# Attention and a SiLU feed-forward on one core: where additions, squares, a transpose and a small matmul stand in the late couples

## The chip, the core and the metric

The kernel runs on one core of one Trainium2 chip. The metric is device time in microseconds (us) of one execution. The kernel before took 1332.61 us (median of three runs, 1331.04 to 1333.44).

## What is computed

```python
def rmsnorm(x, g):
    rms = np.sqrt(np.mean(x * x, axis=-1, keepdims=True) + 1e-06)
    return x / rms * g
q_n, k_n = (rmsnorm(q, g_q), rmsnorm(k, g_k))        # (8, 12, 448, 64): batch, heads, rows, width
scores = 1.0 / np.sqrt(64) * np.matmul(q_n, k_n.transpose(0, 1, 3, 2))
attn = softmax(scores)                                # over the last axis
x = np.matmul(attn, v)                                # then (B, H, S, D) -> (B*S, H*D) = (3584, 768)
h = x @ w_in                                          # (768, 2048)
g = h * (1.0 / (1.0 + np.exp(-h)))                    # SiLU
out = g @ w_out                                       # (2048, 768)
```
All of it is in fp32.

## The kernel before

**Couples.** The 96 heads of all batches are taken four at a time, as 24 *couples* (c = 0 to 23); six couples make a *group*, which is two batches. For each couple the main loop, at the end of `bounded`, calls `visit(c)` and then `between(c)`. I call the second a *stretch*. `GROUP` is 6 and `LATE` is 12.

**A visit** holds the attention of couple c. `scores(c, j, i)` makes four 64x64 matmuls into a PSUM tile named `sc`, of which there are two (L712), and ACT takes the exponential (L717), with the norm of k as its scale. `weigh` multiplies the exponentials with v into two PSUM banks named `av` (L749). The weighing of couple c - 1 ends in the visit of c: first `weigh(c - 1, LEFT)` and the first half of `weigh(c - 1, LEFT - 1)`, then `turn(1, ...)`, a copy of one column into a bank of `av` (L725; on ACT to couple 6, later on DVE), then `scores(c, 0, 1)`, then the second half of that weighing, for which PE waits on the copy. Then `divide` (L807, DVE) takes the result out of `av`, and the weighing of c starts in the same banks. Near the end two additions of exponentials (L763, `add(c, 1)`) go to DVE, and SP issues the loads of v.

**A stretch** holds two calls of `fill`. Each `fill` takes some 14 matmuls out of a generator that makes the products of the first feed-forward layer (L898), and deals other work between them. A list `others` is dealt evenly over the matmuls. A list `prompt` gives its first piece before the first matmul and one more after every third (`HW` is 3). What is dealt is put into its engine's queue at that point of the program, and each engine works its own queue in order.

**The products.** The first layer works by Strassen's scheme in Winograd's form: seven products, each of three matmuls of 128x128 with 448 columns, in the order 1, 2, 6, 5, 7, 3, 4, for each of eight blocks m of a group (`Seven`). The products take two PSUM banks named `mm` in turn, so a product needs that the one two before it has been taken out. ACT takes 1 and 5 out (L906, L916), DVE the others (L856); POOL makes two additions (L918, L919), and the eviction of product 3 reads what L918 wrote. Once the second product of a block has begun, ACT makes SiLU of the block before (L1036) and SP stores it (L931). A couple takes 28 matmuls of the 21 per block, so the stretches of three couples in a row start at three places in a block: couples 12, 15, 18, 21 at product 1, couples 13, 16, 19, 22 within product 6, couples 14, 17, 20, 23 within product 7.

**Late couples.** From couple 12 on q and k are transposed on DVE in place of PE (`flip`: L655 for q, L658 for k), k is scaled afterwards on ACT (`gain`, L664), and q's norm is made on the loaded tile: ACT squares (L672) and DVE adds (L673) in `sum_squares`; then `scale` joins the partial sums of partition pairs with a matmul against a constant (L684), DVE takes it out of its `sc` tile (L685), POOL raises it to the power -1/2 (L688) and multiplies q with it (L691). For k, `normalise` squares on ACT (L467), adds on DVE (L468, L492) and takes the power on POOL (L496), in two pieces, the second of which also issues the loads of the next k on SP (L282, L284).

**The order of a late stretch.** First q's transpose of couple c + 1 and the load of the next q. In the first `fill`: the evictions and the additions of the other exponentials (L763, four pieces) with the pieces of k of couple c + 2. In the second: the matmuls that sum the exponentials (L783), two reciprocals (L792) with the DMAs that spread them (L798, L800), k's transpose, then `gain` and `sum_squares(c + 2)` together. After both, and after the last products of a group with the sums of x (L853) that the next group needs, `scale(c + 2)`. Last comes a tiny exponential on ACT (L1501), ahead of which its table is loaded.

Of the kernel before, what the change touches and what calls it, by code (L numbers as in the profile page):

```python
# [13 lines left out]
ALU = mybir.AluOpType  # L14
# [521 lines left out]
def bounded(  # L536
# [3 lines left out]
    P, D, R, J, S = z.P, z.D, z.R, z.J, z.S  # L540
# [9 lines left out]
    GROUP, LATE = z.NPAIR, z.LATE  # L550
# [33 lines left out]
    n = 2 * room.COLS  # L584
# [13 lines left out]
    def q_of(c):  # L598
        return rows_q[c % 2 if c < GROUP else 0]
# [52 lines left out]
    def flip(c, name):  # L652

        if name == "q":
            nc.vector.transpose(qT.rearrange("p i s -> p (i s)"), q_of(c)[:, 0 : z.NK])  # L655
            load_q(c + 1)
            return
        nc.vector.transpose(kT, place["k1"])  # L658
        if c + 1 < NC:
            loads["quarters"](c + 1)  # L660
# [17 lines left out]
    def scale(c):  # L678

        if c >= NC:  # L680
            return
        f = norm.rms[c % 2][:, 0:n]
        t = ps.tile([P, 2, BANK], F32, name="sc", bufs=2)[:, 0, 0:n]
        nc.tensor.matmul(t, ident, f, start=True, stop=True)  # L684
        nc.vector.tensor_scalar(  # L685
            out=f, in0=t, scalar1=1.0 / D, scalar2=1e-6, op0=ALU.mult, op1=ALU.add
        )
        nc.gpsimd.tensor_tensor(out=f, in0=f, in1=minus_half.to_broadcast([P, n]), op=ALU.pow)  # L688
        rows = q_of(c)[:, 0 : z.NK].rearrange("p (n e) -> p n e", e=z.Q)
        factor = f.rearrange("p (n one) -> p n one", one=1).to_broadcast([P, n, z.Q])  # L690
        nc.gpsimd.tensor_tensor(out=rows, in0=rows, in1=factor, op=ALU.mult)  # L691

    def pair_up():

# [8 lines left out]
    def scores(c, j, i=None):  # L703


        two = ps.tile([P, 2, BANK], F32, name="sc", bufs=2)
        for half in range(2):
            pair = half if j == LEFT else i
            keys = kT[:, ds((z.KA, z.KB)[0 if j == LEFT else i] + j * P, P)]
            for h in range(2):  # L710
                rows = ds(h * D, D)
                nc.tensor.matmul(  # L712
                    two[ds(half * D, D), h, 0:S], keys[rows, ts(half, D)], qT[rows, pair, :],
                    start=True, stop=True,
                )
        for h in range(2):
            nc.scalar.activation(  # L717
                eleft[:, h] if j == LEFT else weights(c, j)[:, i, h], two[:, h, 0:S], AF.Exp,
                scale=norm.column(c, i, h, j),
            )  # L720
# [90 lines left out]
    def normalise(c):  # L811


        def piece(name, i):
            t = scratch[i if c < GROUP + 2 else 0]
            source = raw_of(c) if c < GROUP else q_of(c)
            if name == "q":
                norm.squares_q(c, source, t, i)
            else:
                norm.squares_k(c, place["k0" if c >= LATE else f"k{c % 2}"], t, i)  # L820
            if name == "q" and c < GROUP:
                norm.root(c, name, i)
                norm.scale(c, source, q_of(c), i, nc.gpsimd)
                if i == 1 and c + 2 < GROUP:
                    load_q(c + 2)
            elif i == 1:
                norm.root(c, name)
                if name == "q":
                    for m in range(2):
                        norm.scale(c, source, q_of(c), m, nc.gpsimd)  # L830
                elif LATE <= c < NC - 1:
                    loads["k"](c + 1)

        if c >= NC:
            return []
        return [lambda a=a: piece(*a) for a in (("q", 0), ("q", 1), ("k", 0), ("k", 1))]
# [539 lines left out]
    def weights_in(c, half):  # L1376
        i = 2 * (c - GROUP) + half
        work = [step_of[step] for step in ("ro" if c < GROUP else halves.get(i, ""))]
        return work + [lambda a=a: sum_w_in(*a) for a in sums_halves.get(i, ())]
# [11 lines left out]
    def visit(c):  # L1391

        beside = normalise(c + 1) if 0 < c <= GROUP else []
        if c < NC:
            scores(c, 0, 0)
        if c == 0:
            normalise_alone(1)
        run_all(beside[0:1])
        if c > 0:
            weigh(c - 1, LEFT)  # L1400
            weigh(c - 1, LEFT - 1, 0)
            turn(1, nc.scalar.copy if c <= GROUP else nc.vector.tensor_copy)
        if c < NC:
            scores(c, 0, 1)
        if c > 0:
            weigh(c - 1, LEFT - 1, 1)
            if c - 1 < EARLY:
                for i in range(2):
                    nc.vector.tensor_copy(x_of(c - 1, i), sums[i])
                run_all(beside[1:2])  # L1410
                if inverting:
                    if c > 1:
                        divide(c - 2, None)
                    run_all(inverting)
                    inverting.clear()
            else:
                divide(c - 1, sums)
                run_all(beside[1:2])
                if c < NC and c % GROUP == 0:
                    for i in range(0 if c == GROUP else 1, HW):  # L1420
                        sum_x(last_two(c), i)
                weights_in_visit(c)
            if c + 1 < NC:
                loads["vrest"](c + 1)
        if c == NC:
            return
        scores(c, 1, 0)
        scores(c, 1, 1)
        if c < GROUP:
            run_all(beside[2:3])  # L1430
        weigh(c, 0, 1)
        scores(c, 2, 0)
        weigh(c, 1, 1)
        turn(0, nc.scalar.copy)
        if c < GROUP:
            run_all(beside[3:4])
        scores(c, 2, 1)
        weigh(c, 0, 0)
        run_all(add(c, 1))
        weigh(c, 1, 0)  # L1440
        scores(c, LEFT)
        if c + 1 < NC:
            loads["v"](c + 1)

    def run_all(work):
        for piece in work:
            piece()

    def between(c):

        def transposes_and_sums():
            summing = sum_up(c)
            if c < GROUP:
                next(summing)
            if c < LATE - 1:
                transpose_k(c + 1)
            reciprocals = next(summing)
            if LATE - 1 <= c < NC - 1:
                reciprocals += [lambda: flip(c + 1, "k"), gain]
            if GROUP // 2 <= c <= EARLY:  # L1460
                divide(c - 1, None)
            return reciprocals

        if c < LATE - 1:
            transpose_q(c + 1)
        elif c < NC - 1:
            flip(c + 1, "q")
        if c < GROUP // 2:
            inverting.extend(transposes_and_sums())
        elif c == GROUP - 1:  # L1470
            run_all(transposes_and_sums())
        if c >= GROUP and c % GROUP == 0:
            fetched = range(AHEAD) if c == GROUP else ()
            columns = products - 2 * HW * S * len(fetched)
            work = halves_in(last_two(c), range(HF), plain_in, dict(begun), fetched)
            begin(work, columns, 2 * GROUP)
            begun.clear()
        late = add(c, LEFT - 1) + add(c, LEFT) if c >= GROUP else []
        further = normalise(c + 2) if c >= GROUP - 1 else []
        fill(late + weights_in(c, 0) + further[2:])  # L1480
        prompt = transposes_and_sums() if GROUP // 2 <= c != GROUP - 1 else []
        if c == GROUP // 2:
            begin(make_ahead([0, 1]), AHEAD * 2 * HW * S, GROUP - 1)
        if c >= LATE - 2:
            if c == LATE - 2:
                prompt.append(pair_up)
            queries = prompt[3:] + [lambda: sum_squares(c + 2)]
            fill(weights_in(c, 1), prompt[:3] + [lambda: run_all(queries)])
        else:
            fill(weights_in(c, 1) + (further[:2] if c >= GROUP else []), prompt)  # L1490
        if c % GROUP == GROUP - 1:
            finish()
            if c == GROUP - 1:
                begun[0] = fetch_ahead([0, 1], 0)
            else:
                sum_x([c // GROUP * 2, c // GROUP * 2 + 1], 0)
        if c >= LATE - 2:
            scale(c + 2)
        if GROUP <= c < NC - 1:

            nc.scalar.activation(first, minus_half, AF.Exp)  # L1501
        if c == NC - 1:
            while rounder.load():
                pass

    begun, inverting = {}, []
    load_q(2)
    for _ in range(2):
        room.w_in.load()
# [231 lines left out]
```

## Time and profile before

| What | Value |
|---|---|
| median of three runs | 1332.61 us |
| the profiled execution's own time | 1332.12 us |
| its span, first to last instruction | 1330.3 us |
| granted TensorE clock | 0.998 |
| ACT exponentials L717 | 324 x 632 ns |
| DVE additions L763 (`work` alone) | 114, mean 1117 ns |
| DVE reductions of k's and early q's squares L468 | 56, mean 641 ns |
| POOL powers L496 (128x14 and others) | 43, mean 2467 ns |
| POOL powers L688 (128x28) | 12, mean 4794 ns |
| PE idle before L712, released by L685 | 1.2 us in 2 waits |

Engines are PE (TensorE matmuls), PEld (its weight loads), DVE (VectorE), ACT (ScalarE), POOL (GpSimd) and SP (SyncE, which issues most DMAs). A row of a timeline gives the start in us, the duration in us, engine, line, operation, what it writes and reads, shapes, how many rows are merged, and in brackets the engine's idle time just before it with what ended it. The ends of matmuls are modelled; their starts are recorded. An fp32 matmul shows as two rows.

### The profile page before, as it was taken

Reading aid. Unit: us, or ns where it says so; the run is one execution under the profiler, and the core shown is the slowest. Engines: PE = TensorE matmul, PEld = TensorE weight load, DVE = VectorE, ACT = ScalarE, POOL = GpSimd, SP = SyncE. Lnnn points to the kernel's source line nnn. Section 1 sums busy time; section 2 is a strip of 40 time slices with the busy share of each in tenths; the row PEclk is TensorE's granted clock in tenths of the full one; section 3 lists DMA queues with packets and bytes.
Section 4 is the critical chain, followed back from the end, with each engine's and each line's share of the span. In section 5 each row is a group of like instructions: output and inputs, shape, how many; then the busy total and the mean of one; then the engine's idle time right before and its main releaser. Section 6 shows DMA issues by size and latency. Waiting matters only on the chain.

```text
span 1330.3 us, 19794 instructions
## 1 busy us (share of the span) xinstructions
PE 1299.0 (98%) x7193; PEld 831.3 (62%) x7193; DVE 945.7 (71%) x1629; ACT 505.4 (38%) x886; POOL 361.3 (27%) x227
## 2 busy tenths in 40 slices
PE   8899999999999999999999999999999999999998
PEld 4343444444444444444444455557999999999998
DVE  6787776785755555855554586688978787878785
ACT  7867566645555454455444244410001000001000
POOL 5766534343334333333420154310000000000000
PEclk9999999999999999999999999999999999999999
DMA  9564436233444444444321357522323232332311
GB/s 241 153 178 110 125 90 201 82 91 88 93 113 96 96 95 116 95 92 118 80 67 67 96 176 253 169 72 76 99 76 100 76 105 83 97 103 74 125 50 39
DMA packets 249487, 144.94 MB, mean 109 GB/s; under 512 B 184292, under 2 KB 233316, under 8 KB 249380
## 3 DMA queue, kind: packets, MB, share of 16 engines
q1 hardware_dynamic: 248816, 142.60, 38.3%
q8 instruction: 59, 0.97, 0.3%
q0 software_dynamic: 256, 0.79, 0.2%
q14 instruction: 48, 0.39, 0.1%
q10 hardware_dynamic: 308, 0.20, 0.1%
HBM read 93.98 MB, written 41.29 MB: 102 GB/s over the span
## 4 chain that ended last, share of the span: by engine, by line
PE 83%; DVE 7%; ACT 3%; issue 3%; DMA 2%; POOL 1%; SPq 1%; ACTq 0%; DVEq 0%; POOLq 0%
PE mm L898 26%; PE alone L1205 22%; PE mm L1205 7%; PE av L749 7%; PE alone L898 7%; PE sc L712 7%; PE alone L1242 2%; DVE work L763 1%; DMA work<-work 1%; PE sc L783 1%; DVE work L792 1%; DVE sums_x L853 1%; PE mm L1242 1%; ACT stage L1036 1%; PE sc L647 1%
## 5 line engine op out<-in xcount | busy, mean ns | idle before, releaser
L898 PE MATMUL mm<-x,W 128*128 128x448 f32 x636 | 256.8, 546 | 6.5 <-DVE parts L856 2.7
L717 ACT ACTIVATE work<-sc,rms 128x448 f32<-128x448 f32 x324 | 184.7, 632 | 79.4 <-PE sc L712 62.0
L898 PEld LDWEIGHTS mm<-x,W 128*128 128x128 f32 x636 | 116.7, 190 | 138.6 <-issue 108.8
L898 PE MATMUL mm<-sums_x,W 128*128 128x448 f32 x456 | 183.7, 543 | 1.9 <-DVE parts L856 1.9
L712 PE MATMUL sc<-work 64*64 64x448 f32 x1344 | 165.1, 543 | 2.3 <-DVE rms L685 1.2
L749 PE MATMUL av<-work,rows 64*64 64x448 f32 x1296 | 154.3, 541 | 5.5 <-ACT av L725 1.8
L763 DVE TENSOR_TENSOR work<-work 128x896 f32<-128x896 f32 (+1 forms) x114 | 123.7, 1117 | 50.0 <-PE av L749 49.5
L496 POOL TENSOR_TENSOR rms<-rms,minus_half 128x14 f32<-128x14 f32 (+4 forms) x43 | 106.0, 2467 | 149.5 <-DVE rms L492 140.1
L898 PEld LDWEIGHTS mm<-sums_x,W 128*128 128x128 f32 x456 | 85.0, 190 | 91.0 <-issue 82.7
L523 POOL DMA_DIRECT2D out_dram<-x x2 | 1.3, 653 | 443.2 <-DVE x L856 443.2
L1205 PE MATMUL alone<-W,rows 128*128 128x192 f32 x608 | 113.0, 326 | 0.0
L749 PEld LDWEIGHTS av<-work,rows 64*64 64x64 f32 x1296 | 59.2, 132 | 76.6 <-issue 35.2
L1205 PEld LDWEIGHTS alone<-W,rows 128*128 128x128 f32 x608 | 101.2, 190 | 0.0
L712 PEld LDWEIGHTS sc<-work 64*64 64x64 f32 x1344 | 54.4, 132 | 72.1 <-issue 26.4
L918 POOL TENSOR_TENSOR parts<-parts,stage 128x448 f32<-128x448 f32 x31 | 42.2, 1360 | 148.4 <-DVE parts L856 148.2
L688 POOL TENSOR_TENSOR rms<-rms,minus_half 128x28 f32<-128x28 f32 x12 | 57.5, 4794 | 66.2 <-DVE rms L685 56.9
L1205 PE MATMUL alone<-W,work 128*128 128x192 f32 x382 | 72.2, 326 | 0.0
L1036 ACT ACTIVATE stage<-stage 128x896 f32<-128x896 f32 x63 | 57.3, 945 | 23.0 <-DVE stage L856 22.3
L468 DVE TENSOR_REDUCE rms<-rows 128x8 f32<-128x512 f32 (+2 forms) x56 | 35.9, 641 | 40.3 <-ACT rows L467 37.8
L1205 PEld LDWEIGHTS alone<-W,work 128*128 128x128 f32 x382 | 63.8, 190 | 0.0
L1215 ACT COPY rows<-alone 128x192 f32<-128x192 f32 x34 | 10.8, 318 | 138.0 <-PE alone L1205 79.2
L792 DVE RECIPROCAL work<-sc 128x224 f32<-128x224 f32 x36 | 55.6, 1548 | 4.6 <-PE sc L783 4.4
(247 smaller groups left out, 2114.9 us busy)
## 6 DMA issues: line engine op xcount, KB each, us to landing
hidden<-stage SPq DMA_DIRECT2D x63, 448.0 KB, 3.1
work<-hidden SPq DMA_DIRECT2D x21, 1024.0 KB, 5.1
rows<-in_moe_w_out_dram SPq DMA_DIRECT2D x32, 384.0 KB, 3.5
W<-in_moe_w_in_dram SPq DMA_DIRECT2D x22, 512.0 KB, 5.5
work<-work SPq DMA_DIRECT2D x144, 56.0 KB, 2.0
x<-hidden SPq DMA_DIRECT2D x7, 1024.0 KB, 5.8
rows<-in_q_dram SPq DMA_DIRECT2D x96, 56.0 KB, 2.2
rows<-in_k_dram SPq DMA_DIRECT2D x96, 56.0 KB, 2.3
```

The source lines that it names most:

```text
L496: nc.gpsimd.tensor_tensor(out=t, in0=t, in1=half, op=ALU.pow)
L688: nc.gpsimd.tensor_tensor(out=f, in0=f, in1=minus_half.to_broadcast([P, n]), op=ALU.pow)
L712: nc.tensor.matmul(two[ds(half * D, D), h, 0:S], keys[rows, ts(half, D)], qT[rows, pair, :], start=True, stop=True,)
L717: nc.scalar.activation(eleft[:, h] if j == LEFT else weights(c, j)[:, i, h], two[:, h, 0:S], AF.Exp, scale=norm.column(c, i, h, j),)
L749: nc.tensor.matmul(sums[i][ds(h * D, D), :], v, w, start=(j == 0 and step == 1), stop=(j == LEFT - 1 and step == 1),)
L763: nc.vector.tensor_tensor(out=total, in0=total, in1=more, op=ALU.add)
L792: nc.vector.reciprocal(out=r[0][:, rows], in_=t[:, rows])
L898: nc.tensor.matmul(t, self.left(name, s), self.right(name, s), start=s == ends[0], stop=s == ends[1])
L918: nc.gpsimd.tensor_tensor(out=u2, in0=u2, in1=p5, op=ALU.add)
L1036: nc.scalar.activation(t, t, AF.Silu)
L1205: nc.tensor.matmul(t, x[:, i], y, start=i == ORDER[0], stop=i == ORDER[-1])
L1242: nc.tensor.matmul(o, a[:, 2 * i + m, t], right_one(name, i)[:, m], start=n == 0, stop=n == len(steps) - 1,)
```

## The change

The change touches couples 10 and later.

- `scale(c)` is split: the matmul L684 is issued where it is called, and L685, L688 and L691 are returned as one piece, which `between` runs after the second `fill` and ahead of the group's last products and sums of x.
- k's squares of couple c + 1 move from the stretch of c - 1 into the visit of c, for c from 12 to 22: the first piece after `scores(c, 0, 0)` and ahead of the end of the former couple's weighing with its column copy, the second after the last `weigh` of the visit and ahead of `scores(c, LEFT)`. The loads of the next k move with the second piece.
- In the first `fill`, from couple 12 on, the four additions are dealt as `prompt`, one for every three matmuls, behind q's transpose.
- In the second `fill`, from couple 10 on, the order is: first reciprocal, second reciprocal with its DMAs, `sum_squares(c + 2)`, k's transpose with `gain`, the matmul of `scale(c + 2)`; one for every three matmuls.

```diff
     def scale(c):
         if c >= NC:
-            return
+            return []
         f = norm.rms[c % 2][:, 0:n]
         t = ps.tile([P, 2, BANK], F32, name="sc", bufs=2)[:, 0, 0:n]
         nc.tensor.matmul(t, ident, f, start=True, stop=True)
-        nc.vector.tensor_scalar(
...
+        def roots():
+            nc.vector.tensor_scalar(
+                out=f, in0=t, scalar1=1.0 / D, scalar2=1e-6, op0=ALU.mult, op1=ALU.add
+            )
+            half = minus_half.to_broadcast([P, n])
+            nc.gpsimd.tensor_tensor(out=f, in0=f, in1=half, op=ALU.pow)
...
+            nc.gpsimd.tensor_tensor(out=rows, in0=rows, in1=factor, op=ALU.mult)
+
+        return [roots]
...
     def visit(c):
         beside = normalise(c + 1) if 0 < c <= GROUP else []
+        keys = normalise(c + 1)[2:] if LATE <= c < NC - 1 else []
         if c < NC:
             scores(c, 0, 0)
+        run_all(keys[0:1])
...
         weigh(c, 1, 0)
+        run_all(keys[1:2])
         scores(c, LEFT)
...
         if c < LATE - 1:
             transpose_q(c + 1)
-        elif c < NC - 1:
-            flip(c + 1, "q")
+        turned = [lambda: flip(c + 1, "q")] if LATE - 1 <= c < NC - 1 else [lambda: None]
+        if c == LATE - 1:
+            turned.pop()()
...
-        further = normalise(c + 2) if c >= GROUP - 1 else []
-        fill(late + weights_in(c, 0) + further[2:])
+        further = normalise(c + 2) if GROUP - 1 <= c < LATE - 1 else []
+        if c >= LATE:
+            fill((), turned + late)
+        else:
+            fill(late + weights_in(c, 0) + further[2:])
...
-            queries = prompt[3:] + [lambda: sum_squares(c + 2)]
-            fill(weights_in(c, 1), prompt[:3] + [lambda: run_all(queries)])
+            keys = [lambda: run_all(prompt[2:])]
+            queries = [lambda: sum_squares(c + 2)]
+            joined = [lambda: scaling.extend(scale(c + 2))]
+            fill(weights_in(c, 1), prompt[:2] + queries + keys + joined)
+            run_all(scaling)
+            scaling.clear()
...
-        if c >= LATE - 2:
-            scale(c + 2)
```

More of the change, by code (lines that the diff above doesn't have):

```diff
@@ L684, in scale @@
         nc.tensor.matmul(t, ident, f, start=True, stop=True)
[L685 to L691, printed above, removed]
+        def roots():
[4 more added lines that the diff above has]
+            nc.gpsimd.tensor_tensor(out=f, in0=f, in1=half, op=ALU.pow)
+            rows = q_of(c)[:, 0 : z.NK].rearrange("p (n e) -> p n e", e=z.Q)
+            factor = f.rearrange("p (n one) -> p n one", one=1).to_broadcast([P, n, z.Q])
+            nc.gpsimd.tensor_tensor(out=rows, in0=rows, in1=factor, op=ALU.mult)
+        return [roots]
     def pair_up():
@@ L1504, in between @@
                 pass
-    begun, inverting = {}, []
+    begun, inverting, scaling = {}, [], []
     load_q(2)
```

## Prediction

> **What bounds the kernel.** I read the engine shares and the chain of work first, then the waits, then the timeline of single couples.
>
> ```profile
> PE 1299.0 (98%) x7193; PEld 831.3 (62%) x7193; DVE 945.7 (71%) x1629; ACT 505.4 (38%) x886; POOL 361.3 (27%) x227
> PE 83%; DVE 7%; ACT 3%; issue 3%; DMA 2%; POOL 1%; SPq 1%; ACTq 0%; DVEq 0%; POOLq 0%
> ```
> PE is the clock: what makes it wait is lost, and what runs beside it is free. Matmul ends are modelled, so I counted starts. With no wait, PE rows of 448 columns (or four packed 64x64 ones) start 375 ns apart, so a product of three matmuls (six rows) takes 2.25 us. The visits of couples 11 to 22 start at 298.4, 331.1, 365.4, 399.5, 433.6, 467.2, 501.3, 535.5, 569.7, 603.8, 637.9 and 671.5, some 34 us apart. A visit without waits takes 11.0 us, and the stretch between visits 22.45 (fixed changes of tile shape included). Nearly all are within 1 us of that, so there is little to win. This is what can be won:
>
> ```profile
> 537.77 0.62 DVE L853 TENSOR_TENSOR sums_x<-x,sums_x 128x448 f32<-128x448 f32 x1
> 538.30 0.18 DVE L685 TENSOR_SCALAR rms<-sc 128x28 f32<-128x28 f32 x1
> 538.53 0.98 PE L712 MATMUL sc<-work 64*64 64x448 f32 x8 [0.58 <-DVE rms L685]
> ...
> 415.31 2.46 DVE L763 TENSOR_TENSOR work<-work 128x896 f32<-128x896 f32 x2
> 417.69 0.61 DVE L856 TENSOR_TENSOR stage<-mm,parts 128x448 f32<-128x448 f32 x1
> 418.36 0.30 PEld L898 LDWEIGHTS mm<-x,W 128*128 128x128 f32 x2 [0.85 <-DVE stage L856]
> ```
> First block: at the turn of a group (couples 12 and 18) the sums of x stand ahead of L685, whose PSUM tile the scores need: 0.83 us each. Second: two additions in a row hold an eviction up, 0.40 us. The other place is couples 13, 16 and 19 (below, 0.66 each).
>
> A visit begins like this; these rows decide my forecast:
>
> ```profile
> 434.63 1.16 ACT L717 ACTIVATE work<-sc,rms 128x448 f32<-128x448 f32 x2 [2.34 <-PE sc L712]
> 436.14 0.16 DVE L725 COPY av<-minus_half 128x1 f32<-128x1 f32 x1 [2.26 <-PE av L749]
> 436.64 0.93 PE L749 MATMUL av<-work,rows 64*64 64x448 f32 x8
> ...
> 674.24 0.45 PEld L749 LDWEIGHTS av<-work,rows 64*64 64x64 f32 x8 [0.31 <-DVE av L725]
> ```
> PE's second half of the last weighing (436.64) waits for the one-column copy L725 on DVE; the last row shows that wait by name. Today L725 is done 0.34 us early.
>
> And the second half of a stretch after couple 13:
>
> ```profile
> 391.05 1.28 ACT L1036 ACT_TABLE_LOAD   x1
> 392.34 1.79 ACT L1036 ACTIVATE stage<-stage 128x896 f32<-128x896 f32 x2
> 392.81 0.62 DVE L856 TENSOR_TENSOR stage<-mm,stage 128x448 f32<-128x448 f32 x1 [0.24 <-issue]
> 394.97 0.93 ACT L672 ACTIVATE rows<-rows 128x896 f32<-128x896 f32 x1
> 395.94 1.09 DVE L673 TENSOR_REDUCE rms<-rows 128x28 f32<-128x896 f32 x1 [2.50 <-ACT rows L672]
> 396.94 0.62 DVE L856 TENSOR_TENSOR parts<-mm,stage 128x448 f32<-128x448 f32 x1
> 397.61 1.77 PE L898 MATMUL mm<-x,W 128*128 128x448 f32 x4 [0.39 <-DVE parts L856]
> ```
> L673 waits for ACT's squares and the eviction behind it comes late: the loss here.
>
> [...] rows here overlap by 0.09 to 0.10. [...] L918 takes 1.13 us alone, 1.84 to 1.97 beside an addition.
>
> **The change, part by part.**
>
> *Squares of k into visits 12 to 22.* ACT gets L467 (0.61 to 0.64) after the first pair of exponentials, DVE gets L468 (0.69) after it, in program order ahead of L725. So L725 now waits for ACT. In couple 15: the pair ends at 435.80; square 435.71 to 436.34; reduction 436.37 to 437.06; L725 436.97 to 437.13; PE goes on at 437.19 instead of 436.64. That is 0.55, with a restart about 0.6. Couples 14, 15, 16, 17, 20, 21, 22: 7 x 0.6 = 4.2. (In 14, 17 and 20 the pair ends 0.4 later today because L916 waits for a store; with the stretch before them longer I take the usual time.) In couples 13 and 19 Silu and the table load run into the visit, and the pair ends 3.16 us after its start instead of 2.22: 2 x 1.5 = 3.0. In 12 and 18 it ends at 4.20: a wait of 2.55, against the 0.83 that goes because L685 now stands ahead of the sums: 2 x 1.7 = 3.4. Sum +10.6. Behind L725 stand the divisions L807, which wait for PE anyway. The second square (0.52) fits ACT's wait of 1.1 before the last exponentials; its reduction and L492 put 0.6 on DVE behind the two additions that end the visit.
>
> *That 0.6 at the start of a stretch.* The transpose of q and the first eviction come 0.6 later. In couples 15 and 21 the second product needs that eviction's bank, and it lands at 446.85 against a need at 446.9 to 447.0: no slack, 2 x 0.55 = +1.1. In 12, 13, 16, 18, 19, 22 there is over 0.5 of slack. In 14, 17, 20 the power L496 (2.59 on POOL) now runs to about 4.0 us into the stretch, where L918 stood at 2.4; the eviction waiting for L918 slips by 0.8 and PE stops for 0.55 (nothing to 1.3, if L918 again meets an addition).
>
> *Additions one to a product.* In 14, 17, 20 the stall of 0.40 goes, and without k's reductions ahead of the reciprocals a second of 0.28: with the 0.55, 3 x -0.13 = -0.4. Couple 11 loses its 0.66. In 13, 16, 19 the fourth addition now ends just ahead of the sums. Couple 22 already has that order, and there the sums took 1.18 instead of 0.89 and a later product began 0.17 late: +0.45 each, counted next.
>
> *Squares of q ahead of k's transpose.* After couples 13, 16, 19 the reduction L673 now stands one eviction earlier, ahead of the one at 392.81. It waits for L672, which stands behind the table load and both Silus: with couple 22's clock L672 18.0 to 18.9 us into the stretch, L673 to 20.1, eviction to 20.6. The product that needs its bank is due at 18.9: 1.7, restart 0.1. With the 0.45, less the 0.66 of now: 3 x 1.6 = +4.8. In the other couples L672 is done in time. The transpose and its scaling move some 2 us later; cover is the 1.3 us that the exponential's table then has before the first scores.
>
> *Pair sums inside the stream.* The matmul L684 (28 columns) stands ahead of the last one or two product matmuls. From its start to the next row is 0.23 today, and the trace has no such step between two 128x128 products. Bounds: -0.1 (its gap is paid anyway) and +0.4 (a full reload of weights, 0.19, a slow second row, 0.1, and the 0.1 of a change from product to scores). I take +0.2 for 12 stretches: +2.4.
>
> *SP.* Six loads of k (0.6 each; 3.1 in all) go ahead of v's four and q's eight. Three wait for nothing and use SP's idle time; three follow the second square, so v, q and the store behind come about 1.5 later. q lands at 454 and is squared at 457; L916 waits for a store till 455.4, its bank is needed at 457.1. Nothing; with the cover gone up to 1 us in couples 15 and 21. POOL's L688 and L691 start earlier: nothing.
>
> **Sum.** 10.6 + 1.1 - 0.4 - 0.7 + 4.8 + 2.4 = +17.8. The profiled execution took 1332.12 (span 1330.3, 1.8 around it): 1349.9. The median is 0.5 higher: 1350.4, so 1350.
>
> **Rivals.**
> - Only the visits' wait bites and the stretches come out even: 1332.6 + 10.6 + 0.5 = 1344. For it: PE's product stream has two banks, and DVE is busy only 71%. Against: ACT's order puts L672 behind Silu.
> - More than I see: L918 meets additions (3 x 0.8), L684 at +0.4 (+2.4), the store's cover gone (+2), waits feeding each other: 1358.
> - Faster: the reduction ends before PE needs L725. Place: start of visits; price: the 10.6 and, with L673 in time too, the 4.8 go, leaving the savings of 6 to 7 us less L684's 2.4: 1328.5. It decides at 0.34 us of slack; the square and reduction need 0.9 after the exponentials. L725 would have to be read as not delayed by L468.
> - No effect: the losses halve and the savings cover them: 1332 to 1335.
>
> **Chances.** Forecast (1345 to 1354) 0.53; visits only (1339 to 1345) 0.22; more (1354 to 1364) 0.14; same 0.03; faster 0.08. A measurement of this kernel can tell about 0.2% (2.7 us) from no change. The range 1340 to 1358 leaves out the last two, part of the second's low end and part of the third's high end.
>
> **What would show it.** Right: PE's weighing after L725 waits 0.6 us in most visits and over 1.4 in 12, 13, 18, 19, with L725 behind L468; a wait near 1.8 for the eviction behind L673 after 13, 16, 19; none for L685 in 12 and 18. Wrong: L725 still at 2.6 us into a visit, visits of 11.0 us, or L673 starting with no wait for ACT.

## The result, and the profile after

The changed kernel takes 1353.66 us (median of 6 runs, 1352.89 to 1356.53) against 1333.03 us for the kernel before on the same chip (6 runs, 1330.22 to 1336.57): ratio 1.0161, 95% interval 1.015 to 1.0173. The profiled execution took 1353.88 us with a span of 1352.1, against 1332.12 and 1330.3.

In the changed kernel the lines have moved: scores L717, their exponentials L722, the turning copy L730, weighing L754, additions L768, sums L788, reciprocals L797, products L903, evictions L861, ScalarE's copies L911 and L921, SiLU L1041, table load L1515. L467, L468, L658, L664, L672, L673 and L684 keep their numbers.

The engines' shares:

```profile
PE 1303.3 (96%) x7193; PEld 828.8 (61%) x7193; DVE 944.6 (70%) x1629; ACT 504.3 (37%) x886; POOL 358.1 (26%) x227
```

The same 7193 matmuls, the same counts on every engine: nothing was added, things were moved. TensorE's share fell from 98% to 96%, so the time is in what it waits for. Its waits by what was waited for (us in total, times, longest), first before, then after:

```profile
PE mm L898 <- DVE parts L856: 4.5, 8, 1.4
...
PE mm L898 <- DVE stage L856: 2.2, 2, 1.3
...
PE av L749 <- DVE av L725: 1.5, 1, 1.5
```

```profile
PE av L754 <- DVE av L730: 12.0, 12, 2.5
PE mm L903 <- DVE stage L861: 8.5, 9, 1.6
PE mm L903 <- DVE parts L861: 6.7, 8, 1.7
```

Two waits grew: for the copy that turns the bank (1.5 to 12.0 us, one to twelve times) and for evictions of products (6.7 to 15.2 us). Here is the first, in the visit of couple 15, which starts at 440.76:

```profile
441.81 1.16 ACT L722 ACTIVATE work<-sc,rms 128x448 f32<-128x448 f32 x2 [1.25 <-PE sc L717]
...
442.86 0.63 ACT L467 ACTIVATE rows<-rows 128x512 f32<-128x512 f32 x1
...
443.52 0.69 DVE L468 TENSOR_REDUCE rms<-rows 128x8 f32<-128x512 f32 x1 [4.05 <-ACT rows L467]
...
444.12 0.15 DVE L730 COPY av<-minus_half 128x1 f32<-128x1 f32 x1
...
444.33 0.98 PE L754 MATMUL av<-work,rows 64*64 64x448 f32 x8 [0.33 <-DVE av L730]
```

Exponentials, square, reduction, copy, weighing: each begins where the one ahead of it ends, across three engines. The weighing starts 3.57 us into the visit; before it started 3.06 us in.

The second half of the stretch after couple 13:

```profile
399.19 0.93 ACT L672 ACTIVATE rows<-rows 128x896 f32<-128x896 f32 x1
...
400.16 1.08 DVE L673 TENSOR_REDUCE rms<-rows 128x28 f32<-128x896 f32 x1 [3.24 <-ACT rows L672]
...
401.16 0.61 DVE L861 TENSOR_TENSOR stage<-mm,stage 128x448 f32<-128x448 f32 x1
...
401.83 2.52 PE L903 MATMUL mm<-sums_x,W 128*128 128x448 f32 x6 [1.54 <-DVE stage L861]
```

VectorE waits 3.24 us for squares that stand behind both SiLUs (397.50 to 399.29); the eviction behind the reduction is late, and TensorE stands for 1.54.

And one that I had not foreseen, after couple 15 (the same comes after couple 21):

```profile
464.90 1.56 DVE L797 RECIPROCAL work<-sc 128x224 f32<-128x224 f32 x1 [2.94 <-PE sc L788]
...
466.49 0.62 DVE L861 TENSOR_TENSOR parts<-mm,parts 128x448 f32<-128x448 f32 x1
...
467.17 2.52 PE L903 MATMUL mm<-x,W 128*128 128x448 f32 x6 [1.39 <-DVE parts L861]
```

Product 3 waits for the eviction of product 7, which stands behind a reciprocal. Before, product 3 needed only that product 5 had been taken out: it began at 457.1 and ran on, though product 7 was taken out only at 458.48. The built programs show why: before, the accumulators of couples 13 to 23 take the two banks strictly in turn; in the changed kernel product 3 of couples 15 and 21 has the same bank as product 7.

From start to start on TensorE, by couple (us; visits of 14 to 17 and 20 to 22 before are 10.97 to 11.00):

| | before | after | difference |
|---|---|---|---|
| visits 14 to 17, 20 to 22 | 11.0 | 11.5 to 11.6 | +0.55 to +0.59 each |
| visits 13, 19 | 10.97, 11.00 | 12.80, 12.83 | +1.83 each |
| visits 12, 18 | 11.83, 11.78 | 13.71, 15.14 | +1.88, +3.36 |
| stretches 13, 16, 19 | 23.12 | 24.82 | +1.70 each |
| stretches 15, 21 | 22.67, 22.57 | 25.07, 25.10 | +2.40, +2.53 |
| stretches 14, 17, 20 | 23.14, 23.13, 23.13 | 23.19, 23.19, 23.43 | +0.05, +0.06, +0.30 |
| stretch 23 | 23.53 | 22.33 | -1.20 |

With the small rest (stretches 10, 11, 12, 18: +0.4) this is +22.5, and the spans differ by 21.8. The rest of the kernel makes up the difference: +0.8 ahead of couple 10 and -1.6 behind couple 23, where the trace of before has a drop of TensorE's granted clock (745.69 to 749.11; more on such drops below) and the trace of after has none.

Visit 18 gained 1.5 us more than visit 12 with the same wait (2.46 us for L730 in each). What differs is TensorE's granted clock, the number after the engines in these stretches of 2 us:

```profile
552.00:554.00 2.00, 0.00 (x0) 0.00 (x0) 0.63 (x2) 2.00 (x5) 1.76 (x2) 1.00 0.87 348
554.00:556.00 2.00, 1.82 (x16) 0.71 (x20) 0.68 (x4) 0.39 (x1) 0.00 (x0) 0.70 0.00 0
556.00:558.00 2.00, 2.00 (x16) 0.70 (x12) 1.97 (x5) 1.04 (x2) 0.00 (x0) 0.50 0.26 59
558.00:560.00 2.00, 2.00 (x24) 0.85 (x20) 1.97 (x5) 1.34 (x4) 0.00 (x0) 0.95 0.48 109
```

TensorE starts no matmul from 552 to 554, and then runs at half clock: 2 x (0.30 + 0.50 + 0.05) = 1.7 us of full speed are lost, 3.4 us at half.

### The profile page after: what moved, and what is told of

Read it like the earlier page. It is cut to its first block, busy times and chain, and to the rows that moved or that the text cites. A ratio compares the mean times of both kernels' runs of the same rounds, so it can differ in the third digit from the quotient of the medians.

```text
span 1352.1 us, 19741 instructions
## 1 busy us (share of the span) xinstructions
PE 1303.3 (96%) x7193; PEld 828.8 (61%) x7193; DVE 944.6 (70%) x1629; ACT 504.3 (37%) x886; POOL 358.1 (26%) x227
## 5 line engine op out<-in xcount | busy, mean ns | idle before, releaser
L903 PE MATMUL mm<-x,W 128*128 128x448 f32 x636 | 258.0, 547 | 9.5 <-DVE parts L861 4.2
L722 ACT ACTIVATE work<-sc,rms 128x448 f32<-128x448 f32 x324 | 184.7, 632 | 81.0 <-PE sc L717 66.3
L903 PEld LDWEIGHTS mm<-x,W 128*128 128x128 f32 x636 | 116.5, 190 | 137.6 <-issue 110.3
L903 PE MATMUL mm<-sums_x,W 128*128 128x448 f32 x456 | 185.6, 545 | 7.1 <-DVE stage L861 4.6
L754 PE MATMUL av<-work,rows 64*64 64x448 f32 x1296 | 155.0, 543 | 16.5 <-DVE av L730 12.0
L717 PE MATMUL sc<-work 64*64 64x448 f32 x1344 | 166.1, 547 | 1.1 <-ACT work L722 1.0
L768 DVE TENSOR_TENSOR work<-work 128x896 f32<-128x896 f32 (+1 forms) x114 | 124.9, 1124 | 51.2 <-PE av L754 50.7
L903 PEld LDWEIGHTS mm<-sums_x,W 128*128 128x128 f32 x456 | 84.3, 190 | 96.3 <-issue 78.9
L754 PEld LDWEIGHTS av<-work,rows 64*64 64x64 f32 x1296 | 57.4, 133 | 92.6 <-issue 33.9
L717 PEld LDWEIGHTS sc<-work 64*64 64x64 f32 x1344 | 55.5, 133 | 77.7 <-issue 33.6
L691 POOL TENSOR_TENSOR rms<-rms,minus_half 128x28 f32<-128x28 f32 x12 | 57.5, 4794 | 71.4 <-DVE rms L687 70.2
L468 DVE TENSOR_REDUCE rms<-rows 128x8 f32<-128x512 f32 (+2 forms) x56 | 35.8, 639 | 57.7 <-ACT rows L467 55.6
L797 DVE RECIPROCAL work<-sc 128x224 f32<-128x224 f32 x36 | 55.7, 1549 | 21.4 <-PE sc L788 21.4
L1041 ACT ACTIVATE stage<-stage 128x896 f32<-128x896 f32 x63 | 57.3, 945 | 21.1 <-DVE stage L861 20.3
```

Of the source, the lines that this page charges most:

```text
L691: nc.gpsimd.tensor_tensor(out=f, in0=f, in1=half, op=ALU.pow)
L717: nc.tensor.matmul(two[ds(half * D, D), h, 0:S], keys[rows, ts(half, D)], qT[rows, pair, :], start=True, stop=True,)
L722: nc.scalar.activation(eleft[:, h] if j == LEFT else weights(c, j)[:, i, h], two[:, h, 0:S], AF.Exp, scale=norm.column(c, i, h, j),)
L754: nc.tensor.matmul(sums[i][ds(h * D, D), :], v, w, start=(j == 0 and step == 1), stop=(j == LEFT - 1 and step == 1),)
L768: nc.vector.tensor_tensor(out=total, in0=total, in1=more, op=ALU.add)
L797: nc.vector.reciprocal(out=r[0][:, rows], in_=t[:, rows])
```

## The experiments

Theory: nothing that the change moves costs much in itself. Three instructions stand where something hurried is queued behind them (the reduction L468 ahead of the copy L730; q's reduction L673 ahead of an eviction; k's second reduction and root ahead of q's transpose), and two products fall into the wrong bank. Rival: k's squares in the visits cost by themselves, because ScalarE's exponentials feed TensorE there.

### Taking back one cause at a time

**The reduction behind the copy.** ScalarE's square stays where the change put it.

```diff
+        norm.held = []
         run_all(keys[0:1])
+        held, norm.held = norm.held, None
...
             turn(1, nc.scalar.copy if c <= GROUP else nc.vector.tensor_copy)
+        run_all(held)
```

(`squares` puts its reduction into `held` where there is such a list.)

> The changed kernel with one instruction moved on VectorE alone: in the visits of couples 12 to 22 the reduction of k's first squares is queued behind the copy that turns the bank, not ahead of it; ScalarE still makes those squares at the same place. Theory (the copy waits in VectorE's queue for a reduction that waits for ScalarE): visits 12 to 22 go back to the times of the kernel before, which takes off 0.56 x 7 + 1.85 x 3 + 3.36 = 12.8 us, so about 1341 us, and the granted clock in visit 18 no longer drops, since the idle stretch that preceded the drop is gone. Rival (the visits are longer because ScalarE does 0.62 us of squares ahead of exponentials that TensorE waits for): the visits stay 0.5 us longer each, and the time stays within 2 us of 1353. A second rival for visit 18 (v arrives late behind k's loads): it alone stays 1.7 us long.

Measured: 1344.72 us (1341.93 to 1347.04), ratio to the kernel before 1.0087 (1.0067 to 1.0108). TensorE's wait for the copy, L738 in this kernel, is what it was before:

```profile
PE av L762 <- DVE av L738: 1.5, 1, 1.5
```

The seven visits are back at 10.97 to 11.00, 13 and 19 at 11.42 and 11.37, 12 and 18 at 12.25 and 12.20, with no drop of the clock. ScalarE does the same work in the same order, so the 0.56 of the seven visits is VectorE's queue. The rival keeps 0.4 of visits 12 and 18, and a late v is not what made visit 18 long. The median fell by 8.9 us, the profiled span by 12.0. The granted clocks on record tell why they differ: the four executions took 1341.93, 1343.43, 1346.00 and 1347.04 us with clocks of 0.999, 0.998, 0.995 and 0.995, and the profiled one is the first. By an estimate from these figures, 0.001 of the clock is 0.001 of some 1340 us, or 1.3 us.

**The reduction twice.** The opposite: more ahead of the copy.

```diff
         run_all(keys[0:1])
+        if keys:
+            norm.again(c + 1, scratch[0])
```

(`again` issues L468's reduction once more.)

> The changed kernel with the reduction of k's first squares made twice, both ahead of the turning copy on VectorE, in the visits of couples 12 to 22; ScalarE's work and every transfer are as in the changed kernel. Theory (TensorE waits for the copy that stands behind the reduction): each of the 11 visits grows by the 0.55 us by which VectorE starts one reduction after another (0.69 us long, overlapping its neighbour), +6.1 us, about 1360 us; in visits 12 and 18 TensorE then waits 3.0 us in one piece instead of 2.46, and a drop of the granted clock, 1.5 us each, should follow it more often than in one run of four: 1359 to 1363. Rival (the wait has slack behind ScalarE's exponentials): under 1357.

Measured: 1365.17 us (1364.01 to 1371.33), ratio 1.0266 (1.0247 to 1.0286). The visit of couple 15, starting at 443.79; L484 is the second reduction, L761 the weighing, which waits for the copy L737:

```profile
446.55 0.69 DVE L468 TENSOR_REDUCE rms<-rows 128x8 f32<-128x512 f32 x1 [4.05 <-ACT rows L467]
...
447.27 0.69 DVE L484 TENSOR_REDUCE rms<-rows 128x8 f32<-128x512 f32 x1
...
448.08 0.98 PE L761 MATMUL av<-work,rows 64*64 64x448 f32 x8 [1.05 <-DVE av L737]
```

Every visit grew by what VectorE took longer: 0.72 in this kernel, since the second reduction doesn't start before the first has ended, not the 0.55 that I had expected. Visits 13 and 19 grew by 1.5 us more than that (2.25 and 2.20), because the clock dropped there too (to 0.5), with waits of 2.3 us; in visit 18 (3.2 us) it dropped again, in visit 12 (3.2 us) it did not.

**q's squares behind k's transpose.**

```diff
-            fill(weights_in(c, 1), prompt[:2] + queries + keys + joined)
+            fill(weights_in(c, 1), prompt[:3] + [lambda: run_all(prompt[3:] + queries)] + joined)
```

> The changed kernel with k's transpose and gain put ahead of q's squares and their reduction again, as in the kernel before; the pair-sum product stays inside the stream. Theory (in couples 13, 16 and 19 an eviction stands behind a reduction that waits for squares which stand behind a table load and SiLUs): these three stretches lose about 1.65 us each, so 1349 us. Rival (the stall only moves: the pair-sum product, now inside the stream and right after the reduction, makes TensorE itself wait for the later squares): 1352 to 1356.

Measured: 1352.14 us (1349.51 to 1353.26), ratio 1.0131 (1.0111 to 1.015). Half right: the time is in the rival's range, but not by the rival's cause. Stretches 13, 16 and 19 fell from 24.82 to 23.27, as expected, and visits 13 and 19 by 0.4. But visits 14, 17 and 20 rose from 11.56 to 12.24. The visit of couple 14 starts at 405.68:

```profile
405.48 0.53 ACT L921 COPY stage<-mm 128x448 f32<-128x448 f32 x1 [3.21 <-DMA hidden<-stage]
...
407.43 1.14 ACT L722 ACTIVATE work<-sc,rms 128x448 f32<-128x448 f32 x2
...
409.12 0.69 DVE L468 TENSOR_REDUCE rms<-rows 128x8 f32<-128x512 f32 x1 [4.99 <-ACT rows L467]
```

ScalarE's copy L921 waits for a store to land. The stall of the stretch had covered that; without it, copy and table load reach into the visit, the exponentials start 1.75 us into it instead of 1.05, and the reduction and the copy behind it come 0.7 later. Of 5.5 us, 2.0 came back in another place. Here the clock dropped in visit 12 (15.21) and not in 18 (13.66).

**The banks in turn.**

```diff
-            return ps_mm.tile([P, BANK], F32, name="mm")[:, 0:n]
+            turns["all"] += 1
+            turns["side"] ^= turns["all"] not in (6, 25, 54)
+            return ps_mm.tile([P, BANK], F32, name=f"mm{int(turns['side'])}", bufs=1)[:, 0:n]
```

(At three places ahead of couple 12 two accumulators share a bank in the kernel before, and still do.)

> The changed kernel with the accumulators of successive products placed in the two PSUM banks strictly in turn, as all of couples 13 to 23 have them in the kernel before; nothing else moves. In the changed kernel product 3 of couples 15 and 21 lies in the same bank as product 7, whose eviction stands behind a reciprocal. Theory: the 1.55 us wait in each of these two stretches goes, so about 1350.5 us. Rival (the other bank comes free no earlier, since product 5's copy on ScalarE is late as well): 1353 to 1354.

Measured: 1351.41 us (1349.95 to 1351.87), ratio 1.0133 (1.0116 to 1.015). Stretches 15 and 21 fell to 23.42, by 1.65 and 1.68. Around product 3 of couple 15, with the products at L905:

```profile
464.35 3.27 PE L905 MATMUL mm<-x,W 128*128 128x448 f32 x8
...
466.08 0.62 DVE L861 TENSOR_TENSOR parts<-mm,parts 128x448 f32<-128x448 f32 x1
```

The eviction still stands behind the reciprocal, but product 3 runs on ahead of it: 8 rows without a break. Visit 18 of this kernel also waits 2.46 us for the copy, and there the clock stayed at 1.00 and the visit took 13.66.

**All three at once.**

> The changed kernel with the reduction behind the turning copy, q's squares behind k's transpose and the banks in turn, all at once; the additions stay one to a product, k's squares stay in the visits, the pair-sum product stays in the stream. If the three causes are separate and complete: 1353.7 - 12.8 - 5 - 3.1 = 1332.8, no different from the kernel before (1333.0), and what is left of the change (additions -1.2 at couple 23, pair sums about +0.05 each) may show as up to 2 us below it. If a wait only hides another, it stays above 1338.

Measured: 1336.26 us (1334.25 to 1340.36), ratio 1.0021 (1.0007 to 1.0035). This is 3.5 us above what I had reckoned. The three add up (visits 14, 17 and 20 are at 11.0, their 0.7 included, since nothing waits for that reduction now), but they are not everything. Visits 12 and 18 keep 0.4, and stretches 15 and 21 are at 23.42 against 22.67 and 22.57. At the start of stretch 15 (446.69; L663 is q's transpose, L471 the reduction; the root's first step, 0.18 us, lies between them):

```profile
447.37 0.55 DVE L471 TENSOR_REDUCE rms<-rows 128x6 f32<-128x384 f32 x1
...
448.13 1.11 DVE L663 STREAM_TRANSPOSE work<-rows 128x896 f32<-128x896 f32 x1
...
449.16 0.58 DVE L869 TENSOR_TENSOR stage<-mm,parts 128x448 f32<-128x448 f32 x1
```

The eviction comes 2.47 us into the stretch; before, at 446.27, it came 1.72 in. That is the prediction's "0.6 at the start of a stretch", with 0.75.

### One part alone, in the kernel before

**Pair sums inside the stream.** `scale` is split as in the change, and its product dealt one step behind k's gain and q's squares.

> The kernel before with one part of the change: the pair-sum product stands inside the stream of products (one step after k's gain and q's squares), and what reads it is issued after the stream. Prediction's step: +0.2 us in each of 12 stretches and -0.83 us in visits 12 and 18, whose scores no longer wait for the reading of that product: +0.7 us. Theory now, from the trace of the changed kernel: the two shape changes cost about as much inside the stream as they did at its end, +0.05 to +0.1 us a stretch, and visits 12 and 18 give back 0.6 each: -0.5 to 0 us, so 1332.5 to 1333.5.

Measured: 1333.44 us (15 runs) against 1332.27 (45 runs), ratio 1.0015 (1.0007 to 1.0023). The time lies in the range that I gave, but the difference, +1.2 us where I expected none or a gain, is missed: visits 12 and 18 gave back 0.1, not 0.6, because TensorE then waits for exponentials instead of for L685 (in visit 12 the first of them starts at 334.14, as before at 334.12); stretches 12 and 18 rose by 0.08, 14, 17 and 20 by 0.36, 13, 16 and 19 fell by 0.14. Why the last six differ is not shown. The sum over all couples is +0.9.

**Additions one to a product.**

> The kernel before with one part of the change: in couples 12 to 23 q's transpose opens the stretch's list and the four additions follow one to a product, while k's squares stay in the stretch. Theory: couple 23 loses its 1.2 us (the sums no longer wait for the last addition), couples 14, 17 and 20 may lose up to 0.1 each, nothing else moves: 1332.2 us, -0.1%. Rival (the prediction's +0.45 at couples 13, 16 and 19 and -0.13 at 14, 17 and 20 are real, and couple 23 gained from something else): +1 us, 1334.4.

Measured: 1329.91 us (21 runs), ratio 0.9985 (0.9978 to 0.9992). Stretches 14, 17 and 20 fell by 0.66 each, 13, 16 and 19 rose by 0.29, and stretch 23 fell by 1.20. Both were right in part: the cost in 13, 16 and 19 is real, and the gain is larger than either said. For couple 23, before:

```profile
727.04 1.09 DVE L763 TENSOR_TENSOR work<-work 64x896 f32<-64x896 f32 x1
...
728.18 0.95 PE L783 MATMUL sc<-work,ones 128*32 128x448 f32 x6 [0.27 <-DVE work L763]
```

The last addition was dealt after the first of the sums, which began at 726.97, and the rest waited for it. With the additions one to a product the last two end before the sums, and the sums run through:

```profile
726.87 0.96 PE L783 MATMUL sc<-work,ones 128*32 128x448 f32 x8
```

**k's squares in the visits.**

> The kernel before with one part of the change: k's squares, reductions and roots are made in the visits of couples 12 to 22 for the next couple, the first of them ahead of the turning copy. In the built program this part alone puts product 3 of couples 15 and 21 into product 7's bank. Theory: seven visits +0.56, visits 13 and 19 +1.4, visits 12 and 18 +2.5 less what the earlier reading gave, stretches 15 and 21 +2.4, and perhaps one drop of the granted clock (1.5 us): 3.9 + 2.8 + 4.5 + 4.8 = +16, about 1349 us. Rival (the parts act on each other, and this one alone is cheaper, since q's squares still follow k): under 1343.

Measured: 1354.41 us (1352.44 to 1355.54), ratio 1.0174 (1.016 to 1.0189): as slow as the whole change, and 5 us above the theory. Visits 14, 17 and 20 took +1.11 instead of +0.56 (12.1, near the 12.24 of the kernel with q's squares behind k, an order that this one has too), and stretches 14, 17 and 20 +1.2, which is not there in the whole change, where the additions come one to a product. So this part carries the loss, and the parts are not independent.

**Pair sums and additions together.**

> The kernel before with the two parts that cost nothing: additions one to a product and the pair-sum product inside the stream; k's squares stay in the stretches and q's squares behind k's transpose. If the two add up: 1331.5 to 1332.5 us, 0.1% below the kernel before, with couple 23 shorter by 1.2 us and visits 12 and 18 by 0.6 each. If the reading of the pair sums lands among the additions' evictions and delays one: 1333 to 1335.

Measured: 1330.63 us (14 runs), ratio 0.9992 (0.9984 to 1.0). Couple 23 gained its 1.2 and the additions theirs; visits 12 and 18 only 0.1 each.

### Closing the account

**k's squares out of the way.** In the kernel with q behind k and the banks in turn, the first piece goes behind the division, and the second piece's reduction and root go to the next stretch.

```diff
-        run_all(keys[0:1])
...
                 divide(c - 1, sums)
-                run_all(beside[1:2])
+                run_all(beside[1:2] + keys[0:1])
...
-            fill((), turned + late)
+            fill((), turned + [lambda: run_all(reducing)] + late)
```

> The changed kernel with q's squares behind k's transpose, the banks in turn, and k's squares still in the visits but out of the way: the first piece behind the division, the second piece's reduction and root behind q's transpose in the next stretch. Theory: what the kernel with the three mends still had above the kernel before is visits 12 and 18 (+0.4 each, squares ahead of exponentials on ScalarE) and stretches 15 and 21 (+0.75 each, q's transpose behind the second reduction and root); these 2.3 us go, so 1334 us or less, within 0.1% of the kernel before, and above additions alone. If they stay, their cause is another.

Measured: 1340.94 us (1339.63 to 1341.38), ratio 1.0066 (1.0054 to 1.0079). The two causes went as expected (visits 12 and 18 at 11.95, stretches 15 and 21 at 22.65), and I made a new one: each addition now came one product later, and the sums waited for the last, 1.1 to 1.3 us in each of eight stretches (L796 is the sums, L776 the additions; this is couple 13, where the weights of the sums' last six rows wait and the sums take 1.98 us instead of 0.96):

```profile
389.21 0.15 PEld L796 LDWEIGHTS sc<-work,ones 128*32 128x32 f32 x6 [0.92 <-DVE work L776]
```

**The same with the additions first** (`turned + late + [lambda: run_all(reducing)]`).

> As the kernel with k's squares out of the way, but the second piece's reduction and root follow the four additions instead of standing between q's transpose and them: in that kernel the last addition came one product later and the sums at the middle of the stretch waited for it 0.5 to 1.2 us. Theory: stretches 13, 14, 16, 17, 19, 20, 22 and 23 go back to 23.3, 23.2 (13, 16, 19 and 14, 17, 20), 22.8 and 22.3; stretches 15 and 21 stay at 22.65 and visits 12 and 18 at 11.95; so 1340.9 - 8.2 = 1332.7, no different from the kernel before, and 3 to 4 us above the additions alone without couples 13, 16, 19 and 22. If the root's power on GpSimd, now later, delays a half of an eviction there: up to 0.4 more in 14, 17 and 20.

Measured: 1330.05 us (17 runs, 1328.46 to 1333.24), ratio 0.9984 (0.9976 to 0.9991). Better than expected: stretches 14, 17 and 20 fell to 22.55, as in the kernel with pair sums and additions together, from 23.20 in the kernel with the three mends. Of the change, this kernel keeps the additions one to a product, the pair sums in the stream and k's squares in the visits; the second piece's reduction and root are back in the stretch, q's squares are behind k's transpose again, and the banks are set in turn. It is faster than the changed kernel and than the kernel before, but not than the additions alone (0.9985).

**Additions, but not in couples 13, 16, 19 and 22**, in the kernel before.

> The kernel before with the additions one to a product, but not in couples 13, 16, 19 and 22, which keep the old order: in additions alone stretches 13, 16 and 19 were 0.29 us longer, where the sums' second matmul starts 0.3 us late behind an addition of 1.35 us beside GpSimd. Theory: additions alone less 0.9 us: 1329 us, 0.25% below the kernel before. If the 0.29 came from elsewhere: 1329.9 as for additions alone.

Measured: 1328.72 us (13 runs, 1328.03 to 1330.73), ratio 0.9979 (0.997 to 0.9987), the lowest of all, though its interval overlaps that of the additions alone and that of the kernel above. Stretches 13, 16 and 19 are back at 23.12.

## Why the prediction was right

1353.66 lies in the range, 3.7 above the forecast of 1350; the mechanism named first, L725 behind L468, carries most of the loss. By its terms (us, profiled executions):

| term | predicted | measured | |
|---|---|---|---|
| visits 14 to 17, 20 to 22: L468 ahead of the copy | +4.2 | +4.0 | right; removed and doubled by experiment |
| visits 13, 19 | +3.0 | +3.7 | right; 0.4 each hangs on q's squares |
| visits 12, 18 | +3.4 | +5.2 | right but for 1.5, a drop of the clock; the wait is 2.46, where 2.55 was forecast |
| q's transpose late, couples 15, 21, with L684 | +1.5 | +1.6 | right; 0.75 and 0.85, seen with the bank mended |
| stretches 13, 16, 19, with L684 | +5.4 | +5.1 | right; q behind k takes 4.65 of it away |
| stretches 14, 17, 20, with L684 | +0.2 | +0.4 | right; of it the additions give -2.0 where they stand alone, as reckoned |
| couple 11, with L684 | -0.5 | -0.1 | missed: the stall went, but the sums took 1.34 instead of 0.89 |
| L684 in stretches 10, 12, 18 | +0.6 | +0.5 | right by luck: 0.37 of it is in stretch 10, where L684 is not the cause |
| banks of couples 15, 21 | not named | +3.3 | missed |
| couple 23 | +0 | -1.2 | missed |

The terms that the prediction names come to +20.4 against 17.8, or 18.9 without the drop of the clock. The two that it doesn't name partly cancel, and that the time lies so near the forecast owes something to that.

"Pair sums inside the stream ... I take +0.2 for 12 stretches" was too much where nothing else moved: 0.08 in stretches 12 and 18 alone. The "0.83 that goes" in visits 12 and 18 did not go: with L685 early, ScalarE's exponentials are next late, and alone the edit gave 0.1. "In the other couples L672 is done in time" fails in stretch 10: its +0.37 is -0.14 as soon as q's squares stand behind k's transpose again, with L684 where the change put it. The step for couples 15 and 21 named the late eviction at the start and did not see the bank: I read which products wait from the trace of before and took the placing of their accumulators as given. It follows k's squares, since that part alone shows it too; how the building of the program comes to choose the bank, I did not find out.

The rival "visits only" falls, since the stretches cost 9.7 us in the sum. "Faster" would have needed L730 not delayed by L468; it is what the experiment with the reduction behind the copy makes true, and there the other losses remained. One sign reads lower than forecast: the waits for L730 in most visits are 0.33 us in the profile, not 0.6, as the modelled ends hide part of them; from start to start the weighing is 0.51 later and the visits are 0.56 longer.

What stays open is how building the program chooses a product's bank. In every kernel the time of an execution goes with its granted clock (correlation -0.84 to -1.00 in each set of runs), so a profile of one execution tells the times of stages, and only a median over many tells a difference of 0.2%.

## What to carry to other kernels

An instruction that another engine waits for is as late as the slowest thing ahead of it in its queue, so ask of every small step moved into a phase what is queued behind it and whether it waits for a third engine: here a one-column copy behind a 0.69 us reduction cost 0.55 us in each visit, and the same reduction behind the copy cost nothing. Price a part by where it stands, not by what it is: this change cost 1.6%, and with some of k's squares and sums, q's squares and the banks put elsewhere it ends 0.16% below the kernel before, no more than its additions win alone. When work moves, compare also which buffer each product gets in the built program: two accumulators in one bank cost 1.65 us each time here, about what q's squares cost in a stretch (1.70).

## What the runs showed of the hardware

After some waits of TensorE the granted clock is half for a time. In the changed kernel it is 0.5 from 554.79 to 558.21, 3.41 us, behind the wait of 2.46 us in visit 18; that visit took 15.14 us, and visit 12 with the same wait and no drop 13.71. In the kernel before it is 0.5 from 745.69 to 749.11, behind waits of 1.54 and 1.37 us after the last couple. In the kernel with the reduction twice it fell at 373.73, 561.47 and 599.01, for 3.4 us each time; with the additions alone it was 0.5 for 6.8 us, from 743.4.

The length of a wait doesn't tell whether a drop follows. The clock stayed at 1.00 behind 2.46 us in visit 12 of the changed kernel and in visit 18 of the kernel with the banks in turn, behind 3.2 us in visit 12 of the kernel with the reduction twice, and in the changed kernel behind the same 1.54 and 1.37 us after the last couple.

Where the waits fall in time differs. In three traces the drops lie whole multiples of 3.413 us apart: in the changed kernel the second drop, at the end of the kernel, begins 795.31 us (233 of them) after the first, in the kernel before 583.68 us (171), and in the kernel with the reduction twice the three drops are 187.74 and 37.54 us apart (55 and 11). Counted in such pieces from the first drop of the changed kernel, the 2.46 us of visit 18 lie within one (551.38 to 554.79, TensorE busy for 0.95 us by the modelled ends), and those of visit 12 are split between two (from 332.93, 2.42 and 1.95 us busy). In the kernel before the piece ahead of the drop has 1.27 us busy; but another, from 63.03, has only 1.62 us, and no drop follows. So what decides whether the clock drops is not shown.
